# Regrouping the transfers of an FFT stage in an S4D-plus-GLU kernel

## The chip, the cores and the metric

The kernel runs on one core of a Trainium2 chip. The metric is the device time of one execution in microseconds (us); the time before is the median of three runs. Each profile is one execution recorded by the hardware profiler; times inside it are counted from its first instruction.

## The reference

The input is u (1 x 2048 x 448). It is normalized over its 448 columns and goes into two branches, whose sum with u is the output: an S4D layer (a convolution of 2048 positions, made as a product of spectra, with kernels K made from 256 complex exponentials per column) and a GLU.

```python
x  = A_u
xn = _layernorm(x, axis=-1)

# branch A
dt = jnp.exp(log_dt)
A  = -jnp.exp(log_A_real) + 1j * A_imag
C  = (C_real + 1j * C_imag) * dt[:, None]
P  = jnp.exp((A * dt[:, None])[:, :, None] * pos[None, None, :])
K  = 2.0 * jnp.einsum("dn,dnl->dl", C, P).real          # 448 x 2048
y  = irfft(rfft(xn_t, 2 * L) * rfft(K, 2 * L), 2 * L)[:, :, :L]
a  = y + xn * D_skip

# branch B, F = 1792
g  = xn @ w_gate
b  = (sigmoid(g) * (xn @ w_up)) @ w_down

return x + a + b
```

## The kernel before

Two generators run interleaved, `conv()` (branch A) and `glu()` (branch B). A loop at the end of the kernel always advances the one that has used less of its planned weight (`yield` returns a weight), so the GLU's matmuls fill the gaps that branch A leaves on TensorE. A scheduler in the framework then places the instructions of each engine; `issue_after` and `high_priority` steer it. Each engine works through its own list in order.

Branch A has three parts.

1. `prep` and `x_spec`/`pair_first` (the first 200 us and some of the middle): the parameters, and the first stage of the transform of x, whose rows go to `x1_d` in DRAM: 64 row groups (32 frequencies k, cosine and sine), 64 blocks, 448 columns. The columns of the table `wx` decide in which order the groups lie.
2. `kgen` (to about 580 us): the kernels K in 56 chunks, with a first transform stage (`first_stage`) every four chunks. Its result `sk` (14 banks of 32 columns) goes to `sk_d` in DRAM, by a store in ScalarE's queue (L540).
3. `spectra` (from about 557 us, matmuls from 587 us): the second stage of both transforms, the product, and the way back. It is in two halves of 224 columns (h) with 8 steps each (k in steps of four), 16 steps in all.

A step n of `spectra` does this:

- `back(*prev)` on the products of the step before: 8 matmuls into two PSUM tiles `pv` (L880), two ScalarE copies into `vt` (L886) and four stores of `vt` into `v_d` in DRAM, issued by SyncE (L892);
- `there`: for two pairs of frequencies, matmuls with the kernel rows `skl` and the x rows `sx` against a table `tb` (L854), one ScalarE copy `kc` (L862) and VectorE's complex product into `yy` (L865 to L868);
- `loads` of the step three ahead (`NLD = 3` buffers), issued by SyncE: two loads of x rows `sx` (L826, L827), the table `tb` (L829) and the kernel rows `skl` (L831);
- `turned` (L898): the load of a finished block of `v_d` into `vp`, turned so that positions lie on partitions. `vp` has one buffer for each half in turn, filled by eight such loads;
- once a half is complete, `last(h, m)`: the last stage, 64 matmuls for each two of its four parts m (L909), whose results VectorE adds to `ac` (the first 1024 positions) and `accs` (the others) (L917). `out` (L220) then stores rows to the output, its issues dealt round to SyncE, ScalarE and GpSimd.

For half 0, `last` runs within the steps of half 1; `due` holds the step. For half 1 it comes at the end, behind the last GLU matmuls.

The rotation of the stores, the place of `last` and the dealing are these lines:

```python
                t = wait.pop(0)
                turned(*t)
                if t == (0, 28):
                    due = [n + 1]
```

```python
            eng = (nc.sync, nc.scalar, nc.gpsimd)[outs[0] % 3]
```

The GLU's weights for its last groups are loaded and split by GpSimd (L608, L734, L735, L757, L758); its matmuls are L674 (gate and up) and L781 (down), its ScalarE and VectorE parts L682, L690, L685 and L692.

Of the kernel before, what the change touches and what calls it, by code (L numbers as in the profile page):

```python
# [11 lines left out]
F32 = mybir.dt.float32  # L12
# [8 lines left out]
D = 448  # L21
N = 256
F = 1792
NA = 32
NB = 64
NK1 = 32
# [13 lines left out]
H = D // 2  # L40
# [15 lines left out]
def _tables():  # L56

    a = np.arange(NA)[:, None]
    b = np.arange(NB)[:, None]
    k1 = np.arange(NK1)[None, :]  # L60
    ang = 2 * np.pi * ((a * (4 * k1 + 1)) % 128) / 128.0

    wk = np.zeros((4, NA, 2, 2, NK1))
    wx = np.zeros((4, NA, 2, NK1))
    for j in range(4):
        wk[j, :, 0, j % 2] = wx[j, :, 0] = np.cos(ang)
        wk[j, :, 1, j % 2] = wx[j, :, 1] = -np.sin(ang)

    k2 = np.arange(64)[None, :]
    tab = np.zeros((NK1, 128, 128))  # L70
    for q in range(NK1):
        al = 2 * np.pi * ((b * (4 * q + 1 + 128 * k2)) % 8192) / 8192.0
        c, s = np.cos(al), np.sin(al)
        tab[q] = np.block([[c, -s], [s, c]])
    tab = tab.reshape(8, 4, 128, 128).transpose(0, 2, 1, 3)

    al = 2 * np.pi * ((b * k2) % 64) / 64.0
    split = lambda t: t.reshape(64, 2, 32).transpose(0, 2, 1)
    both = lambda r, i: np.stack([split(r), split(i)], 3).reshape(64, 128)
    bk = np.zeros((2, 64, 2, 128))  # L80
    bk[:, :, 0] = both(np.cos(al).T, np.sin(al).T)
    bk[:, :, 1] = both(-np.sin(al).T, np.cos(al).T)

    wf = np.zeros((2, 2, 4, 8, 32, NA))
    l = 64 * np.arange(NA)[None] + np.arange(64)[:, None]
    for k in range(NK1):
        al = 2 * np.pi * (((4 * k + 1) * l) % 8192) / 8192.0
        wf[:, 0, k % 4, k // 4] = (np.cos(al) / L).reshape(2, 32, NA)
        wf[:, 1, k % 4, k // 4] = (-np.sin(al) / L).reshape(2, 32, NA)

    sel = np.zeros((128, 2, 2, DC, 32))
    st = np.arange(32) + 0.5
    for e in range(DC):
        for i in range(2):
            sel[DC * i + e, 0, 0, e] = st
            sel[64 + DC * i + e, 0, 1, e] = st
            sel[64 + DC * (2 + i) + e, 0, 1, e] = 1.0
    sel[:, 1] = -sel[:, 0]
    for row, tb_, sg in ((16, 1, -1.0), (32, 0, 1.0), (96, 1, 1.0), (97, 0, -1.0)):
        sel[row, 0, tb_] = sg * MAGIC  # L100
    f = lambda v, s: np.ascontiguousarray(v.reshape(s).astype(np.float32))
    return {
        "c_wk": f(wk, (128, 2, 64)),
        "c_wx": f(wx, (128, 64)),
        "c_tab": f(tab, (8, 128, 4, 128)),
        "c_bk": f(bk, (128, 2, 128)),
        "c_wf": f(wf, (128, 32, NA)),
        "c_sel": f(sel, (128, 2, 512)),
        "c_id": np.eye(128, dtype=np.float32),
    }  # L110
# [3 lines left out]
def s4d_glu_kernel(ctx, tc, io):  # L114
    nc = tc.nc
# [6 lines left out]
    dram = ctx.enter_context(tc.tile_pool(name="dram", bufs=1, space=DRAM))  # L122
    acc_d = dram.tile([128, 8, D], F32, name="acc_d")
    ph_d = dram.tile([D, 6, N], F32, name="ph_d")
    x1_d = dram.tile([64, NB, D], F32, name="x1_d")
    sk_d = dram.tile([128, D // 32, 32, 32], F32, name="sk_d")
    wt_d = dram.tile([2, NFT, 128, 8 * 128], F32, name="wt_d")

    v_d = dram.tile([2, 128, 32, H], F32, name="v_d")
    dt_d = dram.tile([2, NFT, 128, D], F32, name="dt_d")  # L130

    const = ctx.enter_context(tc.tile_pool(name="const", bufs=1, side="left"))
# [1 line left out]
    wx = const.tile([128, 64], F32, name="wx")  # L134
    wk = const.tile([128, 2, 128], F32, name="wk")[:, :, :64]
# [75 lines left out]
    def blocks(t, g, b0, nb):  # L211
        return t[g, :, b0 // 8, b0 // 4 % 2, b0 % 4 : b0 % 4 + nb]

    def out(src, b0, h):

        ds = slice(H * h, H * h + H)
        for g in range(4):
            eng = (nc.sync, nc.scalar, nc.gpsimd)[outs[0] % 3]
            outs[0] += 1
            eng.dma_start(blocks(out_t, g, b0, 4)[:, :, ds], src[32 * g : 32 * g + 32, :, ds])  # L220

# [203 lines left out]
    def kgen(pk):  # L425
# [11 lines left out]
        tl = {n: pk.tile(sh, dt_, name=n) for n, sh, dt_ in late}  # L437
# [83 lines left out]
        def first_stage(bank):  # L521

            ks, sk = tl["ks"], tl["sk"].rearrange("p k (s r j) -> p r k s j", r=2, j=2)

            pss = [
                psc[-1].tile([128, 8, 2, 32], F32, name="kp", bufs=1),
                psg.tile([128, 8, 2, 32], F32, name="kq", tag="gu", bufs=4),
            ]
            for s_ in range(8):
                for cc in range(2):  # L530
                    for r in range(2):
                        rows = slice(64 * r, 64 * r + 64)
                        nc.tensor.matmul(
                            pss[r][64 * cc : 64 * cc + 64, s_].rearrange("p j k -> p (j k)"),
                            ks[rows, s_], wk[rows, cc], start=True, stop=True,
                            skip_group_check=True,
                        )
            for r in range(2):
                nc.scalar.copy(sk[:, r], pss[r].rearrange("p s j k -> p k s j"))
            nc.scalar.dma_start(sk_d[:, bank], tl["sk"])  # L540

        with hp(HP):
            phase_load(0)
# [8 lines left out]
        for g in range(NCK // NCH):  # L552
            for c in range(NCH):
# [23 lines left out]
                for q in range(2):  # L577
                    sl = 2 * (cn % 4) + q
                    for k in range(4):
                        h, cc = k // 2, k % 2  # L580
# [222 lines left out]
    def spectra(pf):  # L803
# [18 lines left out]
        def loads(h, k):  # L822
            sx = pf.tile([128, 4, H], F32, name="sx", bufs=NLD)
            sk = pf.tile([128, 7, 4, 32], F32, name="skl", bufs=NLD)
            ds, gs = slice(H * h, H * h + H), slice(7 * h, 7 * h + 7)
            nc.sync.dma_start(sx[0:64], x1_d[k : k + 4, :, ds].rearrange("k b d -> b k d"))  # L826
            nc.sync.dma_start(sx[64:128], x1_d[32 + k : 36 + k, :, ds].rearrange("k b d -> b k d"))  # L827
            tb = pf.tile([128, 4, 128], F32, name="tb", bufs=NLD)
            nc.sync.dma_start(tb, io["c_tab"][k // 4])  # L829

            nc.sync.dma_start(sk, sk_d[:, gs, k : k + 4])  # L831
            return tb, sk, sx

        def bank(name):
# [37 lines left out]
        def back(h, k, ys_):  # L872
            vt = work("vt", [128, 2, 2, H], 2)
            pvs = [bank("pv") for _ in range(2)]
            with after():
                for j in range(2):
                    for e in range(2):
                        for i in range(2):
                            s = slice(64 * i, 64 * i + 64)
                            mm = nc.tensor.matmul(  # L880
                                pvs[i][:, j], bk[s, e], ys_[j][s, e], start=(e == 0), stop=(e == 1),
                                skip_group_check=True,
                            )
            sp_mm[:] = [mm]
            for i in range(2):
                nc.scalar.copy(vt[:, i], pvs[i])  # L886

            for j in range(2):
                for i in range(2):
                    k1 = k + 2 * j + i  # L890
                    to = v_d[h, 8 * (k1 % 4) + k1 // 4 :: 32]
                    nc.sync.dma_start(to.rearrange("r w d -> w r d"), vt[:, i, j])  # L892

        def turned(h, k):
            if h not in vp:
                vp[h] = pf.tile([128, 32, H], F32, name="vp", bufs=1)
            s = slice(k // 4, 128, 8)
            nc.sync.dma_start(vp[h][s], v_d[h, s])  # L898

        def last(h, m):  # L900

            pos = [bank("pv") for _ in range(2)]
            for i in range(2):
                for g in range(4):
                    for b in range(2):
                        s = slice(64 * b, 64 * b + 64)
                        w = 8 * g + m + i
                        with after():
                            mm = nc.tensor.matmul(  # L909
                                pos[b][32 * g : 32 * g + 32, i], wf[s, w], vp[h][s, w],  # L910
                                start=True, stop=True, skip_group_check=True,
                            )
            sp_mm[:] = [mm]
            for b in range(2):
                q, o, ds = 2 * (m // 4) + b, m % 4, slice(H * h, H * h + H)
                acc = ac[:, 4 * q + o : 4 * q + o + 2, ds] if q < 2 else accs[q][:, o : o + 2, ds]
                v.tensor_tensor(acc, acc, pos[b], ALU.add)  # L917
            if m % 4 == 2 and m < 4:
                for q in range(2):
                    out(ac[:, 4 * q : 4 * q + 4], 4 * q, h)  # L920

        ac = acl[0]
        lasts.append(last)
# [7 lines left out]
        for n, (h, k) in enumerate(steps):  # L931
# [18 lines left out]
            while len(wait) > 1 and not (due and wait[0][0] == 1):  # L950
                t = wait.pop(0)
                turned(*t)
                if t == (0, 28):
                    due = [n + 1]
            prev = (h, k, cur)
            glu_on[:] = [1]
            yield WS
# [141 lines left out]
```

## Time and profile before

| | us |
|---|---|
| median of 3 runs | 773.14 (771.35 to 775.21) |
| time of the profiled execution | 770.64 |
| span of the profile (first to last instruction) | 768.9 |
| TensorE busy | 705.4 |
| VectorE busy | 557.4 |
| ScalarE busy | 420.3 |
| GpSimd busy | 359.7 |
| TensorE clock granted, mean | 0.968 of full |

Of the 770.64 us, 1.7 lie outside the span. The transfers move 114.31 MB in 89,575 packets; SyncE's queue carries 92.36 MB of them, ScalarE's 14.57 and GpSimd's 6.17.

How to read the rows quoted below: a timeline row has the start, the time taken, the engine (a "q" behind the engine's name: an instruction of its queue that issues a transfer), the line, the operation and its tiles, the count, and in brackets the idle time before it and what ended it. DVE is VectorE, ACT ScalarE, POOL GpSimd, SP SyncE, PE TensorE.

### The profile page before, as it was taken

What the parts mean: (1) busy time and instruction counts of PE and PEld (TensorE: products, weight loads), DVE (VectorE), ACT (ScalarE), POOL (GpSimd) and SP (SyncE); (2) the same over time, 40 slices, a digit from 0 to 9 for tenths busy, and PEclk for the clock granted to TensorE, in tenths of its full rate; (3) what the DMA queues carried; (4) which work ended last, traced back from release to release, by engine and by line L of the source; (5) the groups of instructions that cost most, each with busy time, mean ns of one, the idle gap of its engine ahead of it and who ended that gap; (6) DMA issues with size and microseconds to landing.
All of it is one profiled execution on the core that took longest, in us unless ns stands there. A gap on an engine that the chain in (4) does not pass through costs nothing.

```text
span 768.9 us, 19294 instructions
## 1 busy us (share of the span) xinstructions
PE 705.4 (92%) x7868; PEld 555.6 (72%) x7868; DVE 557.4 (72%) x768; ACT 420.3 (55%) x647; POOL 359.7 (47%) x423
## 2 busy tenths in 40 slices
PE   2798899997999999898999999999899999969994
PEld 1575688876877877565788887887777778746783
DVE  5779996798978998778478977877864554634553
ACT  3636364767677976777387667686552322312320
POOL 1101036896785788853437584486555002331001
PEclk9998899999999999899999999999999999989998
DMA  9936337334323542363962232222157999999846
GB/s 205 227 81 187 95 93 230 101 122 151 120 70 126 185 135 67 108 189 92 269 182 69 68 124 66 90 94 67 41 142 199 283 240 238 230 241 242 189 127 161
DMA packets 89575, 114.31 MB, mean 149 GB/s; under 512 B 10896, under 2 KB 77456, under 8 KB 89232
## 3 DMA queue, kind: packets, MB, share of 16 engines
q1 hardware_dynamic: 80176, 92.36, 45.3%
q10 hardware_dynamic: 6736, 14.57, 6.3%
q0 software_dynamic: 2576, 6.17, 3.1%
q8 instruction: 62, 1.02, 0.6%
q14 instruction: 25, 0.20, 0.1%
HBM read 69.21 MB, written 43.84 MB: 147 GB/s over the span
## 4 chain that ended last, share of the span: by engine, by line
PE 40%; DMA 16%; DVE 15%; ACT 10%; POOL 9%; issue 7%; SPq 2%; ACTq 1%; POOLq 0%; DVEq 0%
PE gu L674 13%; PE po L781 11%; PE tr L506 4%; PE sp L854 4%; PE ko L582 3%; POOL me L483 3%; PE pv L880 2%; DVE pm L420 2%; DMA sx<-x_d 2%; DVE Et L569 2%; DVE Et L568 2%; ACT S L518 2%; POOL mf L483 2%; DVE Ft L570 2%; ACT S L516 1%
## 5 line engine op out<-in xcount | busy, mean ns | idle before, releaser
L483 POOL TENSOR_TENSOR me<-me,pm 128x32 f32<-128x32 f32 (+1 forms) x168 | 135.5, 807 | 99.5 <-DVE Et L569 88.1
L483 POOL TENSOR_TENSOR mf<-mf,pm 128x64 f32<-128x64 f32 (+1 forms) x112 | 118.0, 1054 | 4.5
L674 PE MATMUL gu<-xh,wh 128*128 128x512 f32 x336 | 101.3, 408 | 5.2 <-ACT xh L201 5.2
L569 DVE TENSOR_TENSOR Et<-me,S 128x1024 f32<-128x1024 f32 x56 | 80.0, 1429 | 24.5 <-ACT me L496 20.0
L674 PE MATMUL gu<-xh,wl 128*128 128x512 f32 x336 | 96.9, 394 | 0.0
L674 PE MATMUL gu<-xl,wh 128*128 128x512 f32 x336 | 96.6, 391 | 0.0
L781 PE MATMUL po<-dh,hh 128*128 128x448 f32 x224 | 87.3, 390 | 4.4 <-DVE acc L786 2.5
L568 DVE TENSOR_TENSOR Et<-me,S 128x1024 f32<-128x1024 f32 x56 | 77.9, 1391 | 16.8 <-ACT S L518 16.6
L690 ACT CAST hh<-hf 128x512 fp32r<-128x512 f32 x56 | 34.9, 623 | 98.9 <-DVE hf L685 74.7
L570 DVE TENSOR_TENSOR Ft<-mf,S 128x1024 f32<-128x1024 f32 x56 | 80.2, 1433 | 9.6 <-ACT S L518 7.4
L781 PE MATMUL po<-dl,hh 128*128 128x448 f32 x224 | 84.7, 379 | 0.0
L781 PE MATMUL po<-dh,hl 128*128 128x448 f32 x224 | 83.7, 376 | 0.0
L515 ACT ACTIVATE S<-tr 128x1024 f32<-128x1024 f32 x56 | 57.6, 1028 | 40.4 <-PE tr L506 34.9
L674 PEld LDWEIGHTS gu<-xh,wh 128*128 128x128 f32 x336 | 62.4, 193 | 22.1 <-ACT xh L201 6.7
L582 PEld LDWEIGHTS ko<-Et,Ft 128*32 128x32 f32 x3584 | 54.8, 112 | 28.4 <-issue 13.7
L674 PEld LDWEIGHTS gu<-xh,wl 128*128 128x128 f32 x336 | 63.2, 189 | 15.2 <-DVE pl L289 0.7
L674 PEld LDWEIGHTS gu<-xl,wh 128*128 128x128 f32 x336 | 63.2, 188 | 14.1 <-issue 0.7
L582 PE MATMUL ko<-Et,Ft 128*32 128x64 f32 x3584 | 64.9, 224 | 9.1 <-DVE Et L568 7.3
L685 DVE SCALAR_TENSOR_TENSOR hf<-th,gu 128x512 f32<-128x512 f32 x56 | 38.1, 681 | 42.3 <-PE gu L674 31.5
L506 PE MATMUL tr<-sel,ph 128*128 128x512 f32 x224 | 66.8, 419 | 1.7 <-ACT S L517 1.1
L786 DVE SCALAR_TENSOR_TENSOR acc<-po,acc 128x448 f32<-128x448 f32 x80 | 48.2, 617 | 24.4 <-PE po L781 24.3
L518 ACT ACTIVATE S<-S,hpi 128x1024 f32<-128x1024 f32 x56 | 65.5, 1169 | 0.0
(190 smaller groups left out, 1299.8 us busy)
## 6 DMA issues: line engine op xcount, KB each, us to landing
sk_d<-sk ACTq DMA_DIRECT2D x14, 512.0 KB
sx<-x_d SPq DMA_DIRECT2D x32, 224.0 KB
skl<-sk_d SPq DMA_DIRECT2D x16, 448.0 KB
v_d<-vt SPq DMA_DIRECT2D x64, 112.0 KB
vp<-v_d SPq DMA_DIRECT2D x16, 448.0 KB
wt_d<-wh SPq DMA_DIRECT2D x9, 512.0 KB
wt_d<-wl SPq DMA_DIRECT2D x9, 512.0 KB
wh<-wt_d SPq DMA_DIRECT2D x9, 512.0 KB
```

What stands on the lines that cost most here:

```text
L483: ins = nc.gpsimd.tensor_tensor(m[:, :, w + a : 2 * w : n], m[:, :, a:w:n], par(base + i).unsqueeze(2).to_broadcast([128, 4 * DC, w // n]) ...
L506: nc.tensor.matmul(ps[:, h], ph[:, cn % 2, 128 * h : 128 * h + 128], sel[:, i], start=(i == 0), stop=(i == 1),)
L515: nc.scalar.activation(rows(cs), pv, AF.Abs)
L518: sins[:] = [nc.scalar.activation(cs, cs, AF.Sin, scale=-TWO_PI, bias=hpi)]
L568: v.tensor_tensor(Et[:, :, :, 32:64], two(me[:, :, 32:64]), S[:, 1::-1], ALU.mult)
L569: v.tensor_tensor(Et[:, :, :, 0:32], two(me[:, :, 0:32]), S[:, 1:3, :, ::-1], ALU.mult)
L570: fts[:] = [v.tensor_tensor(Ft, two(mf), S[:, 3:5], ALU.mult)]
L582: mm = nc.tensor.matmul(ko[32 * j : 32 * j + 32, sl], Ft[:, cc, DC * h + 4 * q + j], Et[:, cc, DC * h + 4 * q + j], start=(k == 0), stop=( ...
L674: glu_mm[:] = [nc.tensor.matmul(ps, a_, b_, start=(n == 0), stop=(n == len(mm) - 1))]
L685: marks[1] = v.scalar_tensor_tensor(hf, th, 1.0, pgu[1], ALU.add, ALU.mult)
L781: glu_mm[:] = [nc.tensor.matmul(po, a_[:, bs], w_, start=(n == 0), stop=(n == 3 * fc - 1))]
L786: v.scalar_tensor_tensor(acc[:, b], po, 0.5, acc[:, b], ALU.mult, ALU.add)
```

## The change

- `v_d` gets the layout [half, block, q, r, 32, columns]. The table `bk` has its columns in another order, so that the partitions of `vt` are (r, w); `vt` is written as [j, i]. The four stores of a step become one of 128 partitions x 4 x 224, and ScalarE issues it, right behind its two copies to `vt`.
- The rows in `x1_d` lie as (k, c) instead of (c, k), by the table `wx`; the two loads of x become one of 128 partitions.
- `sk_d` is laid out by half and step. A load of kernel rows is one contiguous row of 3,584 bytes per partition instead of 7 pieces of 512 bytes; the store of a bank (L540) becomes 8 pieces of 512 bytes per partition instead of one of 4,096.
- `turned` reads four q x four r rows of 28,672 bytes, as large as before.
- The outs of half 0's `ac` rows all go to SyncE; those of half 1 are dealt as before.
- `due` is one step later: the last stage of half 0 moves from the steps n = 10 and 11 to n = 11 and 12.

Bytes, matmuls and the elements that the engines compute are the same.

```diff
     wk = np.zeros((4, NA, 2, 2, NK1))
-    wx = np.zeros((4, NA, 2, NK1))
+    wx = np.zeros((4, NA, NK1, 2))
     for j in range(4):
-        wk[j, :, 0, j % 2] = wx[j, :, 0] = np.cos(ang)
-        wk[j, :, 1, j % 2] = wx[j, :, 1] = -np.sin(ang)
+        wk[j, :, 0, j % 2] = wx[j, :, :, 0] = np.cos(ang)
+        wk[j, :, 1, j % 2] = wx[j, :, :, 1] = -np.sin(ang)
...
-    split = lambda t: t.reshape(64, 2, 32).transpose(0, 2, 1)
-    both = lambda r, i: np.stack([split(r), split(i)], 3).reshape(64, 128)
+    both = lambda r, i: np.stack([r.reshape(64, 2, 32), i.reshape(64, 2, 32)], 2).reshape(64, 128)
...
-    sk_d = dram.tile([128, D // 32, 32, 32], F32, name="sk_d")
+    sk_d = dram.tile([128, 2, 8, D // 64, 4, 32], F32, name="sk_d")
-    v_d = dram.tile([2, 128, 32, H], F32, name="v_d")
+    v_d = dram.tile([2, 8, 4, 4, 32, H], F32, name="v_d")
...
-    def out(src, b0, h):
+    def out(src, b0, h, engs=(nc.sync, nc.scalar, nc.gpsimd)):
         ds = slice(H * h, H * h + H)
         for g in range(4):
-            eng = (nc.sync, nc.scalar, nc.gpsimd)[outs[0] % 3]
+            eng = engs[outs[0] % len(engs)]
...
-            nc.scalar.dma_start(sk_d[:, bank], tl["sk"])
+            to = sk_d[:, bank // 7, :, bank % 7].rearrange("p e k d -> p e (k d)")
+            nc.scalar.dma_start(to, tl["sk"].rearrange("p (e k) d -> p e (k d)", k=4))
...
-            ds, gs = slice(H * h, H * h + H), slice(7 * h, 7 * h + 7)
-            nc.sync.dma_start(sx[0:64], x1_d[k : k + 4, :, ds].rearrange("k b d -> b k d"))
-            nc.sync.dma_start(sx[64:128], x1_d[32 + k : 36 + k, :, ds].rearrange("k b d -> b k d"))
+            ds = slice(H * h, H * h + H)
+            rows = x1_d.rearrange("(k c) b d -> (c b) k d", c=2)
+            nc.sync.dma_start(sx, rows[:, k : k + 4, ds])
             tb = pf.tile([128, 4, 128], F32, name="tb", bufs=NLD)
             nc.sync.dma_start(tb, io["c_tab"][k // 4])
-            nc.sync.dma_start(sk, sk_d[:, gs, k : k + 4])
+            nc.sync.dma_start(sk, sk_d[:, h, k // 4])
...
             for i in range(2):
-                nc.scalar.copy(vt[:, i], pvs[i])
-            for j in range(2):
-                for i in range(2):
-                    k1 = k + 2 * j + i
-                    to = v_d[h, 8 * (k1 % 4) + k1 // 4 :: 32]
-                    nc.sync.dma_start(to.rearrange("r w d -> w r d"), vt[:, i, j])
+                nc.scalar.copy(vt[:, :, i], pvs[i])
+            to = v_d[h, k // 4].rearrange("q r w d -> (r w) q d")
+            nc.scalar.dma_start(to, vt.rearrange("p j i d -> p (j i) d"))
...
-            s = slice(k // 4, 128, 8)
-            nc.sync.dma_start(vp[h][s], v_d[h, s])
+            src = v_d[h, k // 4].rearrange("q r w d -> r q (w d)")
+            nc.sync.dma_start(vp[h][k // 4 :: 8].rearrange("p w d -> p (w d)"), src)
...
-                    out(ac[:, 4 * q : 4 * q + 4], 4 * q, h)
+                    out(ac[:, 4 * q : 4 * q + 4], 4 * q, h, *([] if h else [[nc.sync]]))
...
                 if t == (0, 28):
-                    due = [n + 1]
+                    due = [n + 2]
```

## The prediction

> **What bounds the kernel now.** I read the page's busy times, then the stretches of the last 170 us (the only part whose order of work changes), then what TensorE waited for there, then the timelines of TensorE, ScalarE and SyncE around the longest wait, and the chain of waits for what a transfer takes.
>
> ```profile
> span 768.9 us, 19294 instructions
> ## 1 busy us (share of the span) xinstructions
> PE 705.4 (92%) x7868; PEld 555.6 (72%) x7868; DVE 557.4 (72%) x768; ACT 420.3 (55%) x647; POOL 359.7 (47%) x423
> ```
>
> TensorE is busy for 92% of the span, so only its idle time can be won. By stretch (length, TensorE busy with its count, granted clock, share of the transfer engines, GB/s):
>
> ```profile
> 600.00:660.00 60.00, 60.00 (x444) 1.00 1.09 243
> 660.00:680.00 20.00, 19.58 (x149) 1.00 1.05 233
> 680.00:700.00 20.00, 12.11 (x120) 0.83 1.01 252
> 700.00:720.00 20.00, 19.45 (x187) 1.00 0.94 222
> 720.00:740.00 20.00, 20.00 (x156) 1.00 0.58 148
> ```
>
> The transfer engines are full from 600 to 700 us, yet TensorE doesn't stop until 680; there it loses 7.89 us of 20. Its waits after 580 us (total, times, longest):
>
> ```profile
> PE pv L909 <- DMA vp<-v_d: 7.3, 1, 7.3
> PE pv L880 <- DMA bk<-in_c_bk_dram: 1.4, 1, 1.4
> PE sp L854 <- ACT vt L886: 1.1, 1, 1.1
> PE pv L909 <- issue: 0.9, 1, 0.9
> PE pv L909 <- DVE pd L866: 0.6, 1, 0.6
> ```
>
> So one wait matters: the last stage of the first half of the columns (L909) stands for the transfer of vp. TensorE's timeline (start, us, what) shows where:
>
> ```profile
> 656.90 1.78 PE L880 MATMUL pv<-yy,bk 64*128 64x224 f32 x16
> ...
> 667.01 1.78 PE L880 MATMUL pv<-yy,bk 64*128 64x224 f32 x16
> ...
> 674.62 1.78 PE L880 MATMUL pv<-yy,bk 64*128 64x224 f32 x16
> ...
> 678.66 0.93 PE L854 MATMUL sp<-sx,tb 128*64 128x224 f32 x8
> 686.84 3.26 PE L909 MATMUL pv<-vp,wf 64*32 64x224 f32 x64 [7.25 <-DMA vp<-v_d]
> ...
> 701.43 1.72 PE L909 MATMUL pv<-vp,wf 64*32 64x224 f32 x48
> 703.70 0.96 PE L909 MATMUL pv<-vp,wf 64*32 64x224 f32 x16 [0.56 <-DVE pd L866]
> ```
>
> The same 64 matmuls cost 3.26 us behind the wait, where the clock fell to 0.83, but 48 of them 1.72 us later, which is 2.29 for 64: the wait also costs 0.97 of clock. ScalarE shows the third piece:
>
> ```profile
> 658.72 0.97 ACT L886 COPY vt<-pv 128x448 f32<-128x448 f32 x2 [0.37 <-PE pv L880]
> ...
> 692.92 5.21 ACTq L220 DMA_DIRECT2D out_dram<-ac  x3
> 698.17 0.62 ACT L690 CAST hh<-hf 128x512 fp32r<-128x512 f32 x1 [18.72 <-DMA out_dram<-ac]
> ```
>
> Three stores of out stand in ScalarE's queue, wait for the late last stage, and hold up the copies behind them; that is the 1.06 us TensorE waits for vt (1.1 in the list).
>
> And SyncE shows why vp was late:
>
> ```profile
> 666.56 3.51 SPq L892 DMA_DIRECT2D v_d<-vt  x4
> ...
> 675.96 0.51 SPq L898 DMA_DIRECT2D vp<-v_d  x1
> ...
> 745.55 2.46 SPq L892 DMA_DIRECT2D v_d<-vt  x4
> 748.06 0.60 SPq L220 DMA_DIRECT2D out_dram<-acc  x1
> 750.22 0.54 SPq L898 DMA_DIRECT2D vp<-v_d  x1
> ```
>
> The last block of the first half was in vt at 659.69 (658.72 + 0.97). SyncE, busy in order with the loads of later steps, issued its four stores 6.87 us later, from 666.56, and its load, behind the next step's loads, at 675.96; it landed 10.88 us after that, at 686.84. In the chain of waits, from issue to landing:
>
> ```profile
> 659.16 6.77 DMA v_d<-vt
> ...
> 666.00 8.57 DMA vp<-v_d
> ```
>
> **The change part by part.**
>
> *Later last stage.* The last stage of half 0 moves one step on: in the changed order, 22 gate matmuls, the backward matmuls and the next forward matmuls come first. That stretch is what lies between 656.90 and 667.01, so TensorE arrives at 679.59 + 10.11 = 689.7, where before it arrived at 679.59. Even with the old transfers (landed 686.84) the wait would be gone. Removed: 7.25 of wait and 0.97 of clock. What is late next at this place is a PSUM bank: the first 64 matmuls then meet VectorE's reads as the second 64 did, so I add 0.56 once more; the bounds are 0 and twice that.
>
> *Store of v from ScalarE.* Per step, four issues leave SyncE and one appears on ScalarE, between the copies to vt and the copy kc. An issue there costs:
>
> ```profile
> L540 ACTq DMA_DIRECT2D sk_d<-sk x14: 326/327/375, 191.5 to 583.0; - x14
> ```
>
> So 0.33 us, 16 times 5.2 us on ScalarE. Behind it wait kc, then VectorE's products, then the next backward matmuls. VectorE can't begin before the matmuls on x are done, one group after those that kc reads, and this covers most of 0.33. VectorE's slack is thinnest where few GLU matmuls fill a step:
>
> ```profile
> 673.85 0.39 DVE L868 TENSOR_TENSOR yy<-pd 128x224 f32<-128x224 f32 x1
> ```
>
> It ends 0.38 us before the matmuls at 674.62, and the second half of those is needed still later. I take 0.2 in all, with 0 and 5.2 (no cover at all) as the bounds.
>
> The store also has a wait of its own. In both orders each transfer of SyncE and ScalarE waits for the one eight places earlier, and with five transfers a step instead of nine that is, for a store of v in the first half, the vp load of two steps earlier. From one store to the end of that load: 0.33 + 6.77 + 0.51 + 8.57 = 16.2 us, with the slow load of 10.88 18.5 us. Two steps (656.90 to 674.62) are 17.72 us. So a store blocks ScalarE by 0 to 0.8 us, at most six times: 0 to 4.7 us, and it must still eat through the slack above. I take 0.4.
>
> *Outs of half 0 from SyncE alone.* Three issues leave ScalarE's queue and two GpSimd's: the 1.06 us go. SyncE then issues eight in a row behind the last stage; only the loads of the sixteenth step and the second half's vp stand behind them. Even ten us of that are free: that step's forward matmuls come more than three steps later, 26.6 us at 17.72 for two. Nothing added.
>
> *SyncE's own order* becomes: kernel rows, vp, x, table. The x load now stands behind a load that waits for the store of v, landing 0.97 + 0.33 + 6.77 = 8.1 us after the backward matmuls. The x load is used three steps after those (26.6 at 8.86 a step); 26.6 - 8.1 - 0.5 leaves 18 us for a transfer, where vp's took 8.57. Hidden.
>
> *Row sizes.* A kernel load is 128 rows of 3,584 B instead of 896 of 512 B, for 512-byte rows in the 14 stores of sk, which run while the engines are half idle. No row of before separates transfers by row size, so I take nothing: below, 16 loads quicker by some tenths each that TensorE doesn't wait for; above, the same in the stores.
>
> [...]
>
> *End.* The last vp is issued at 750.22, after four stores that took 2.46 us to issue. One store from ScalarE, ready with the copies, should free 0.5 of the 0.86 us that the last stage waits ("issue" 0.9 in the list); bounds 0 and 0.86.
>
> *bk.* Its load (1.4) has somewhat fewer SyncE transfers beside it; I take 0, bounds 0 and 1.4.
>
> Sum: -7.25 - 0.97 - 1.06 + 0.56 + 0.2 + 0.4 - 0.5 = -8.6 us. The profiled run took 770.64 us (span 768.9); the runs shown have a median of 773.14 (771.35 to 775.21), so against the median **764.5 us**.
>
> **The rivals.**
>
> *1. Late loads.* The new order on SyncE delays x and the table more than they can bear. For it: the queue is a chain in which each waits for a landing. Against: 18 us of room. It needs landings twice as long; then about half of the gain goes: **769**.
>
> *2. The transfer engines are the bound.* The share of 1.05 to 1.09 up to 680 means that they lag, and the wait at L909 is only where the lag shows; bytes don't change, so 7.25 and 0.97 come back at the loads of the next steps, and 1.06 alone is won: **772**. Against: TensorE's list holds not one wait on x, table or kernel rows, and the engines have 0.06 and 0.42 of two 20-us stretches free right after, 9.6 us.
>
> *3. Slower: ScalarE blocks on its stores.* The loop store, vp load, next-but-one store closes over ScalarE's queue. It decides once store plus load exceed two steps, 17.72 us. If whole stores of 448 KB take twice 6.77, the loop takes 0.33 + 13.54 + 0.51 + 8.57 = 22.95 us, 2.6 us more a step, and with six such steps 15.7 us: 764.5 + 15.7 = **780**. For it: the loop stands at 16.2 already. Against: the four stores of before shared SyncE's queue with all loads, and the same bytes landed in 6.77.
>
> **How the numbers follow.** Forecast 0.74, late loads 0.07, full engines 0.10, blocked ScalarE 0.09. The forecast's own range is 761.6 (no bank wait, nothing on ScalarE, the end and bk at their best: 0.56 + 0.6 + 0.36 + 1.4 less) to 768 (3.5 us more on ScalarE, whose bounds allow 9.3). With two us of scatter of the runs and the late loads, 760.5 to 770 holds 8 in 10. About 0.5% (3.9 us) is what a measurement of this kernel can tell from no change: faster 0.78 (the forecast and half of the late loads), same 0.13, slower 0.09.
>
> **What would show it.** Right: TensorE's waits after 595 us name no vp before the end; in 680 to 700 us it is busy for over 19 us at a clock of 1.00; SyncE issues the eighth vp before 670 us; ScalarE has no idle time ended by a transfer; the waits on a PSUM bank at the last stage are about 0.6 twice. Wrong: idle time of ScalarE at vt or kc that is ended by vp or v_d (rival 3), waits of the forward matmuls on x, table or kernel rows (rivals 1 and 2).

## The result, and the profile after

The changed kernel takes 807.19 us (805.45 to 810.48, 4 runs) beside 773.79 us of the kernel before (771.35 to 775.21, 4 runs): a ratio of 1.044, 95% interval 1.0395 to 1.0485. The forecast was 764.5. The profiled execution took 806.23 us. In the changed kernel the load of vp is L894, the store of v L888, the last stage L905 and the outs L219.

The page after, first lines:

```profile
span 804.4 us, 19179 instructions
...
PE 718.4 (89%) x7868; PEld 560.5 (70%) x7868; DVE 560.5 (70%) x768; ACT 420.1 (52%) x647; POOL 358.8 (45%) x421
```

TensorE has 13.0 us more of busy time for the same 7868 matmuls (its mean granted clock was 0.947, against 0.968), and 22.5 us more of idle time (804.4 - 718.4 = 86.0, against 63.5). Nearly all of both lies behind 600 us, as the stretches show (length, busy time with its count of each engine, sums, granted clock, share of the transfer engines, GB/s):

```profile
600.00:680.00 80.00, 71.68 (x476) 53.18 (x472) 36.06 (x70) 16.26 (x32) 9.32 (x11) 0.91 0.78 186
680.00:740.00 60.00, 52.07 (x440) 37.36 (x440) 29.37 (x56) 14.77 (x29) 11.01 (x13) 0.94 0.77 201
740.00:804.00 64.00, 40.71 (x350) 31.63 (x346) 21.56 (x42) 7.08 (x14) 4.42 (x8) 0.81 0.40 122
```

From 600 to 680 us before had TensorE at work for 60.00 + 19.58 us, with the transfer engines at a share of 1.09 and 1.05. Now they carry less, 0.78 and 186 GB/s, and TensorE stands all the same: over all 16 engines together it isn't that there is too much to move. Waits after 540 us, of TensorE, then of VectorE, of ScalarE, and of SyncE's queue (total, times, longest):

```profile
PE pv L880 <- DVE yy L867: 12.7, 7, 4.0
PE pv L905 <- DMA out_dram<-acc: 12.5, 1, 12.5
PE sp L854 <- ACT vt L886: 3.4, 2, 2.3
PE pv L880 <- DVE yy L868: 2.2, 2, 1.7
```

```profile
DVE yy L865 <- ACT kc L862: 65.4, 13, 9.1
```

```profile
ACT kc L862 <- DMA vp<-v_d: 16.7, 3, 6.4
```

```profile
SPq L894 <- DMA v_d<-vt: 87.0, 12, 24.9
```

The 7.3 us of the last stage on vp are gone. In their place TensorE waits nine times, 14.9 us, for VectorE's products, VectorE for ScalarE's kc, and kc for a load of vp that it doesn't read: its engine stood before the issue of a store. ScalarE's timeline has the place:

```profile
647.73 0.97 ACT L886 COPY vt<-pv 128x448 f32<-128x448 f32 x2 [6.34 <-PE pv L880]
654.61 0.37 ACTq L888 DMA_DIRECT2D v_d<-vt  x1
655.08 0.97 ACT L862 COPY kc<-sp 128x448 f32<-128x448 f32 x2 [6.38 <-DMA vp<-v_d]
```

The store could have left at 648.70; it left at 654.61, and kc behind it. The chain of waits gives the loop and its terms (start, time taken, what):

```profile
616.33 3.22 DMA v_d<-vt
...
619.57 20.31 DMA vp<-v_d
...
639.95 5.16 DMA v_d<-vt
...
645.13 20.11 DMA vp<-v_d
...
665.32 6.12 DMA v_d<-vt
...
671.45 23.01 DMA vp<-v_d
...
694.54 0.37 ACTq L888
...
739.36 19.29 DMA v_d<-vt
```

Store, load, next-but-one store: 616.33, 639.95, 665.32, 694.54. Each of the last three stores left as the load of vp eight places ahead of it in the two queues had landed (619.57 + 20.31 = 639.88, 645.13 + 20.11 = 665.24, 671.45 + 23.01 = 694.46); in before the load of the table at 674.59 stands in the same way behind the load of vp at 666.00 (666.00 + 8.57 = 674.57). A loop takes 26.07 us on average, where two steps of before took 17.72. Three loops cost 3 x 8.35 = 25.1 us; in the second half the slow store at 739.36 holds vt for 7.3 us, and at the end the last stage waits 12.5. Less the 7.25 + 0.97 + 1.06 that did go, that makes 35.6, and the two profiled executions differ by 806.23 - 770.64 = 35.6. That it comes out to the tenth is luck: the terms are waits of different engines (of the 7.3 us at vt TensorE lost 2.3), and the lower clock behind the waits has no term of its own. The row of the 12.5 us names a store of out, which the last stage doesn't read; it reads the last block of vp, whose load left at 777.01 and whose rows, by the trace's records of single rows, moved until 789.17. That this load set the wait is the likely reading; the row doesn't show it.

The 20.1 to 23.0 us of a vp load, where before had 8.57, are the new fact. They are the time from issue to landing, and the loads come in pairs. SyncE's timeline has the first pair:

```profile
616.47 0.54 SPq L894 DMA_DIRECT2D vp<-v_d  x1
...
619.57 0.53 SPq L894 DMA_DIRECT2D vp<-v_d  x1
```

By the records of single rows, the first of these loads moved from 619.09 to 629.98, and the second began at 632.32 and moved for 7.0 us. The other two pairs look the same: the second load's own rows took 8.5 and 10.9 us, where three loads of before took 6.0 to 6.6. So a third to a half of the 20 us is the load itself, and most of the rest is spent behind the vp load that was issued 3.1 to 3.3 us ahead of it.

At the end of each kernel a load of vp is nearly alone. The stretches (columns as in the prediction), first of before, then of after:

```profile
751.50:753.50 2.00, 2.00 (x12) 1.00 0.97 229
```

```profile
784.00:789.00 5.00, 0.00 (x0) 0.50 0.23 92
```

The same 448 KB keep 0.97 x 16 = 15.5 transfer engines busy before and 0.23 x 16 = 3.7 after. Such a share counts a row's whole time in the stretch in which the row starts, so it gives the count only where the stretch holds that time (a quarter of a microsecond of before, from 751.50, shows 5.85). The records of single rows agree with the count: before, 16 rows start within 0.6 us and take 1.3 to 2.4 us each, so 16 are under way at once; after, never more than four are in this stretch, and each new one starts as another ends. The new load reads its 16 rows in two dimensions, four r and four q, that can't be merged into one; before read them in one dimension of 16.

So the first theory, A: the outer dimension of the load's source sets how many transfer engines carry it, here four. The rivals: B, the single store of v, or its place in ScalarE's queue, is what costs, as the prediction's third rival had it; and C, any read order other than that of DRAM is slow, however many engines it uses.

### The profile page after: what moved, and what is told of

Its sections match the earlier page's. It is cut to its first block, busy times and chain, and to the rows that moved or that the text cites. A ratio compares the mean times of both kernels' runs of the same rounds, so it can differ in the third digit from the quotient of the medians.

```text
span 804.4 us, 19179 instructions
## 1 busy us (share of the span) xinstructions
PE 718.4 (89%) x7868; PEld 560.5 (70%) x7868; DVE 560.5 (70%) x768; ACT 420.1 (52%) x647; POOL 358.8 (45%) x421
## 4 chain that ended last, share of the span: by engine, by line
PE 39%; DMA 21%; DVE 14%; POOL 9%; ACT 8%; issue 7%; SPq 1%; ACTq 1%; POOLq 0%; DVEq 0%
PE gu L674 16%; PE po L781 9%; DMA vp<-v_d 8%; DMA v_d<-vt 4%; PE tr L505 4%; POOL me L482 4%; PE ko L582 3%; POOL mf L482 2%; PE sp L854 2%; DVE pm L419 2%; PE pv L880 2%; DVE Et L568 2%; DVE Et L569 2%; ACT S L517 2%; DVE Ft L570 1%
## 5 line engine op out<-in xcount | busy, mean ns | idle before, releaser
L674 PEld LDWEIGHTS gu<-xh,wl 128*128 128x128 f32 x336 | 63.5, 190 | 15.3 <-DVE pl L288 0.7
L865 DVE TENSOR_TENSOR yy<-kc,sp 128x448 f32<-128x448 f32 x32 | 19.7, 616 | 75.0 <-ACT kc L862 65.4
```

What stands on the lines that cost most here:

```text
L674: glu_mm[:] = [nc.tensor.matmul(ps, a_, b_, start=(n == 0), stop=(n == len(mm) - 1))]
```

## Experiments

**The read order alone, taken back and put in.** In the changed kernel the load reads its rows in DRAM's order:

```diff
-            src = v_d[h, k // 4].rearrange("q r w d -> r q (w d)")
+            src = v_d[h, k // 4].rearrange("q r w d -> (q r) (w d)")
```

> The changed kernel, but the vp load reads its 16 rows of 28,672 bytes in the order in which they lie in DRAM (one dimension of 16) instead of in the order r, q (4 x 4, which don't merge into one). Bytes, row sizes, queues and waits are the same; the rows land on other partitions, so the result is permuted. Theory A (a load whose source is 4 x 4 rows is served by 4 of the 16 engines, each with four rows one behind the other; this makes vp's 20 us and, through the wait of v's store for the load two steps earlier, blocks ScalarE): vp lands in 6 to 11 us, ScalarE isn't stopped by a transfer, 762 to 768 us. Theory B (stores of v in ScalarE's queue are slow to land or block it by themselves, whatever the load does): no change against the changed kernel, 800 to 808 us.

Measured: 768.08 us (761.61 to 770.31, 10 runs), ratio to before 0.993 (0.9895 to 0.9965): the upper end of what A expected. TensorE's waits after 540 us:

```profile
PE pv L880 <- DVE yy L868: 2.6, 2, 1.3
PE ko L582 <- DVE Et L568: 2.5, 1, 2.5
PE pv L880 <- DMA bk<-in_c_bk_dram: 2.1, 1, 2.1
PE pv L905 <- DVE pd L866: 0.5, 2, 0.3
```

39 us come back by the order of 16 rows. The waits for products are down to 2.6 us from 12.7 + 2.2, and none names a transfer of v; no wait of ScalarE's names a transfer either. The store still stands in ScalarE's queue, so B is not what costs 33 us. Then the reverse, in the kernel before:

```diff
-            nc.sync.dma_start(vp[h][s], v_d[h, s])
+            src = v_d[h].rearrange("(r q e) w d -> e q r (w d)", r=4, q=4)[k // 4]
+            nc.sync.dma_start(vp[h][s].rearrange("p w d -> p (w d)"), src)
```

> The kernel before, but its vp load takes the same 16 rows in the order q, r (4 x 4, not mergeable); the result is permuted, nothing else is changed: stores of v from SyncE, last stage at its old place. Theory A: vp takes about 20 us instead of 8.6 to 10.9, the wait at the last stage grows from 7 to 18 us or more, and SyncE, which waits eight transfers back, holds up loads too: 785 to 810 us. Theory B: 773 us, no change, since no store is in ScalarE's queue.

Measured: 831.35 us (827.2 to 834.29, 4 runs), ratio 1.0742 (1.0674 to 1.081): the order alone, with nothing else of the change, costs more than the whole change did. The direction is A's; the size was missed by over 20 us, and the wait for vp at the last stage of the first half stayed near its 7.25 us instead of growing to 18. TensorE's largest waits, and ScalarE's:

```profile
PE pv L910 <- DMA out_dram<-acc: 25.3, 1, 25.3
PE sp L854 <- ACT vt L886: 21.7, 7, 5.9
PE pv L910 <- DMA vp<-v_d: 7.5, 1, 7.5
```

```profile
ACT vt L886 <- DMA v_d<-vt: 57.2, 8, 10.6
```

Here nothing of ScalarE's stands behind a store. The stores themselves land late (8.23 to 12.08 us in the chain of waits, against 6.77 in before), and vt's buffers come free late. The one vp load in that chain takes 11.27 us, not the 20 that A expected.

**How many engines.** Two more read orders in the changed kernel, first 8 x 2, then 2 x 8:

```diff
-            src = v_d[h, k // 4].rearrange("q r w d -> r q (w d)")
+            src = v_d[h, k // 4].rearrange("q r w d -> (q r) (w d)").rearrange("(a b) x -> b a x", a=2)
```

> The changed kernel with the vp load reading the 16 rows in an 8 x 2 order instead of 4 x 4 (the result is permuted by it). Theory A (the size of the outer dimension of the source sets how many of the 16 transfer engines carry the load: 4 with 4 x 4, 8 with 8 x 2): 2 rows for an engine instead of 4, a load of some 9 to 13 us, a total of 768 to 778. Theory B (any order other than that of DRAM is slow, by two dimensions as such): 800 to 808, with loads of 20 us.

> The changed kernel with the vp load reading the 16 rows in a 2 x 8 order instead of 4 x 4 (the result is permuted by it). Theory A (the size of the outer dimension of the source sets how many transfer engines carry the load: 16, 8, 4 and here 2): 8 rows for an engine, a load of some 35 to 45 us where 8 x 2 took 9.5 in the chain of waits and 4 x 4 took 20.1 to 23.0, a loop of some 20 to 25 us a step and a total of 880 to 980. Theory B (4 x 4 is slow for another reason, such as the distance of 28,672 bytes between the rows that follow each other): at most as slow as 4 x 4, 807 or less.

Measured: 8 x 2 took 770.29 us (one run, before 773.34), within A's 768 to 778; 2 x 8 took 841.75 us (one run, before 770.89). The chain of waits of 8 x 2, then of 2 x 8:

```profile
667.65 9.50 DMA vp<-v_d
```

```profile
606.60 11.85 DMA v_d<-vt
618.46 14.05 DMA vp<-v_d
...
678.44 16.28 DMA vp<-v_d
694.80 16.31 DMA v_d<-vt
```

And a stretch at the end of 2 x 8, in which only rows of vp move:

```profile
810.00:812.00 2.00, 0.00 (x0) 0.50 0.13 57
```

0.13 x 16 = 2.1 engines, against 3.7 with 4 x 4 and 15.5 with one dimension of 16. For 8 x 2 the last load of vp shows it by its rows, which start in two groups:

```profile
748.50:749.00 0.50, 0.50 (x4) 1.00 1.83 459
749.00:749.90 0.90, 0.90 (x6) 1.00 0.00 0
749.90:751.00 1.10, 1.10 (x7) 1.00 0.88 209
```

459 GB/s for 0.50 us and 209 for 1.10 are 8 rows of 28,672 bytes each; the second eight start as the first eight end. So 8 engines carry it. This is A's count in all four orders, and C falls: 8 x 2 is no more in DRAM's order than 4 x 4, and its one time is within the runs of the load in DRAM's order (761.61 to 770.31). But the total of 2 x 8 was expected at 880 to 980, from loads of 35 to 45 us; they took 14 to 16. In these stretches an engine moved more where few ran: 57 GB/s / 2.1 = 27 GB/s each, 92 / 3.7 = 25, but 229 / 15.5 = 14.8. A single row took 1.06 us with two under way and 1.07 with four, but 1.9 with eight and with sixteen. From the start of its first row to the end of its last, a load with almost nothing beside it took 2.6 us on 16 engines, 4.3 on 8, 5.4 on 4 and 8.6 on 2. From 8 to 4 that is 1.1 us more, while in the loop the one stopped ScalarE once, for 4.3 us, and cost nothing that its time shows, and the other cost 33 us: the count alone doesn't price the loss. What the other transfers add on the few engines that the load uses was not measured apart. And with two engines more of the loop sits in the stores, 11.85 to 16.31 us here against 3.22 to 6.12 with 4 x 4: each row of the chain counts the time to its own landing, and what one kernel books on the load the other books on the store.

What is shown is the count for four orders of this one load: 16, 8, 4 and 2 rows under way at once, with an outer dimension of 16, 8, 4 and 2. What sets it for other transfers was not shown.

**Who passes it on.** The changed kernel with its 4 x 4 load, the store moved to SyncE:

```diff
-            nc.scalar.dma_start(to, vt.rearrange("p j i d -> p (j i) d"))
+            nc.sync.dma_start(to, vt.rearrange("p j i d -> p (j i) d"))
```

> The changed kernel with its 4 x 4 load of vp, but the store of v issued by SyncE. Theory A (the load alone is the cause; the store in ScalarE's queue is only the place where its slowness is passed on): no gain or a small one, 795 to 815, and the idle time ended by v_d or vp is found at vt or at the forward matmuls instead of at kc. Theory B (the prediction's third rival as written: ScalarE blocks because its store waits for a load two steps back, and without that the slow load hides): kc no longer waits for vp, 765 to 780.

Measured: 837.92 us (one run, before 770.89). Both were wrong on the size; of A's signs, the idle time at vt that a store of v ends is there. With this load the store was cheaper in ScalarE's queue than in SyncE's, by 30 us. TensorE's and ScalarE's waits:

```profile
PE pv L905 <- DMA out_dram<-acc: 26.2, 1, 26.2
PE sp L854 <- DMA tb<-in_c_tab_dram: 16.1, 4, 7.0
PE sp L854 <- issue: 14.5, 2, 7.6
```

```profile
ACT vt L886 <- DMA v_d<-vt: 63.3, 8, 10.0
```

Now that SyncE issues store and load, the tables of later steps come late: the prediction's first rival, which the change as it stands did not show. With a load that uses all engines, does the store's queue matter at all? Both of these give v the old order of `bk`, rows (r, q), one store of 32 x 16 x 224 a step and a load of 16 rows; they differ in the engine that issues the store:

```diff
-            to = v_d[h, k // 4].rearrange("q r w d -> (r w) q d")
-            nc.scalar.dma_start(to, vt.rearrange("p j i d -> p (j i) d"))
+            to = v_d[h, k // 4].rearrange("r q w d -> w r q d")
+            nc.sync.dma_start(to, vt.rearrange("p j i d -> p (j i) d"))
...
-            src = v_d[h, k // 4].rearrange("q r w d -> r q (w d)")
+            src = v_d[h, k // 4].rearrange("r q w d -> (r q) (w d)")
```

> The changed kernel with a store and a load of v that both go over 16 rows: v_d is written as (r, q) rows in the old order of bk, one store a step of 32 x 16 x 224, issued by SyncE and not by ScalarE; the load of vp reads 16 rows in their order. Theory A (the 4 x 4 read order of the vp load is what cost, and a store in ScalarE's queue some us besides): as fast as the changed kernel with v's transfers as before, 760 to 763 us, no idle time of ScalarE ended by a transfer. Theory B (one large store a step is itself slow, wherever it stands): 768 or more, with landings of the store well over the 6.77 us of the four small ones.

> The same kernel as the one with a single store of 32 x 16 x 224 from SyncE, but with the store issued by ScalarE. Theory A (ScalarE's queue, where the store stands ahead of kc, costs some us): 765 to 768 us, 4 to 6 above the one from SyncE, with TensorE waiting for VectorE's products. Theory B (the layout of the store matters and its queue does not): the same as from SyncE within 2 us.

Measured: from SyncE 764.84 us (756.07 to 766.59, 6 runs), ratio 0.9877 (0.9834 to 0.9919); from ScalarE 765.66 us (762.07 to 770.94, 9 runs), ratio 0.9909 (0.9877 to 0.994). The intervals overlap: a single store in ScalarE's queue costs nothing that these runs can tell, and the 4 to 6 us that were expected for it are not there. 764.84 lies between what A and B expected for the store from SyncE (760 to 763, and 768 or more), so it decides less than the pair does. Four stores in that queue are another matter. This version keeps the new order of `bk`, and has four stores a step by r and a load of 16 rows:

```diff
-            nc.scalar.dma_start(to, vt.rearrange("p j i d -> p (j i) d"))
+            for r in range(4):
+                to = v_d[h, k // 4, r].rearrange("q w d -> w q d")
+                nc.scalar.dma_start(to, vt[32 * r : 32 * r + 32].rearrange("p j i d -> p (j i) d"))
```

> The changed kernel, correct, with rows in DRAM in the order r, q: the load is 16 rows in one dimension, and the store of a step becomes four (one for each r) of 32 partitions x 4 x 224, still from ScalarE. Theory A: 763 to 770 us; four issues cost ScalarE 1.5 us a step, mostly covered. Theory B: at or above the changed kernel, 800 us or more, since ScalarE now has four stores a step to wait with.

Measured: 776.45 us (773.23 to 783.52, 10 runs), ratio 1.0063 (1.0021 to 1.0104), outside both expectations. TensorE's wait, and ScalarE's timeline:

```profile
PE pv L880 <- DVE yy L867: 6.5, 6, 2.4
```

```profile
657.22 3.36 ACTq L889 DMA_DIRECT2D v_d<-vt  x4
660.67 0.97 ACT L862 COPY kc<-sp 128x448 f32<-128x448 f32 x2 [3.49 <-issue]
```

Four issues and their waits take 3.4 us ahead of kc, where one takes 0.37: VectorE's slack covers the one and not the four.

**The other parts of the change.** All of it but v's transfers:

> The changed kernel with its v part undone (layout, table order, four stores a step from SyncE, load of 16 rows as before); merged load of x, large kernel rows, outs from SyncE and the later last stage stay. Theory A and theory B both say that the loss goes: the 7.25 us wait, its 0.97 us of clock and ScalarE's 1.06 us are won, 762 to 768 us. If one of the other parts costs by itself (theory C: 512-byte stores of sk, or SyncE's outs), it stays above 773.

Measured: 761.58 us (761.21 to 768.28, 4 runs), ratio 0.9865 (0.9797 to 0.9932). That another part of the change costs (theory C) is not borne out. Then its two parts alone, first the last stage and the outs (the new parameter of `out` and its call are as in the change):

```diff
-            eng = (nc.sync, nc.scalar, nc.gpsimd)[outs[0] % 3]
+            eng = engs[outs[0] % len(engs)]
...
-                    due = [n + 1]
+                    due = [n + 2]
```

> The kernel before with only two edits of the change: the last stage of half 0 one step later, and the outs of half 0 from SyncE alone. All transfers are as before. The prediction's terms for these two were -7.25 - 0.97 - 1.06 + 0.56 = -8.7 us: 764.4 against the median of 773.1 shown there, 762 to 767. Rival (full transfer engines, the prediction's second rival): the time comes back at later loads, 770 to 772.

Measured: 766.92 us (760.09 to 775.7, 12 runs), ratio 0.992 (0.9886 to 0.9953). The last stage no longer waits for vp, and the interval leaves out the rival's 770 to 772. Then the loads alone (the `loads`, `wx` and `sk_d` parts of the diff), and of these the kernel rows alone:

> The kernel before with only the regrouped loads of x and of the kernel rows (with their layouts in DRAM); v's transfers, the last stage and the outs are as before. The prediction took nothing for these: 773, within 3 us of before, TensorE still waiting some 7 us for vp at the last stage of the first half. Rival (fewer instructions in SyncE's queue let the vp load leave earlier and shorten that wait, which is what the version with v's transfers as before had over the one with only the later last stage, 761.6 against 766.9): 766 to 769, with that wait at 4 or less.

> The kernel before with the kernel rows alone regrouped: a load is one row of 3,584 bytes a partition instead of seven of 512, and the store of a bank has pieces of 512 bytes; the two loads of x, v, the last stage and the outs are as before. Theory A (512-byte rows kept the transfer engines busy longer for the same bytes, and the wait for vp at the last stage came of that): share of the transfer engines from 600 to 680 us at 0.90 as in the version with both loads regrouped, where before had 1.08; the wait for vp gone or under 2 us; 763 to 767 against a before of 771 to 773. Theory B (fewer issues in SyncE's queue let vp leave earlier): share still above 1.0, the wait for vp still 5 us or more, 770 to 774.

Measured: both loads 764.68 us (759.11 to 769.39, 12 runs), ratio 0.9916 (0.9884 to 0.9948); kernel rows alone 765.76 us (760.91 to 769.73, 12 runs), ratio 0.9929 (0.9895 to 0.9964). In both the wait for vp is gone; the prediction had given them nothing. The stretch from 600 to 680 us, of the version with both, of that with the kernel rows alone, and of the later last stage:

```profile
600.00:680.00 80.00, 79.00 (x579) 1.00 0.89 255
```

```profile
600.00:680.00 80.00, 80.00 (x592) 1.00 1.06 266
```

```profile
600.00:680.00 80.00, 80.00 (x590) 1.00 1.08 257
```

The kernel rows alone give the time of theory A without its sign, a share of 0.90: it stayed at 1.06, as B had it, while B's time and its wait did not come. SyncE's timeline there has the eighth load of vp:

```profile
669.46 0.51 SPq L899 DMA_DIRECT2D vp<-v_d  x1
```

That is 6.5 us earlier than the 675.96 of before, with as many issues in the queue as before. But one profile each can't put this down to the rows: counted from its first backward matmuls, the eighth load left after 81.87 us in before, after 74.78 here, and after 76.73 in the version with the later last stage alone, whose loads are those of before. How larger rows win their 5.3 us is open. And a share of 1.06 to 1.08 doesn't mean that the engines are full: 266 and 257 GB/s pass at 1.06 and 1.08, and 255 at 0.89.

The two parts take away the same wait, and don't add up: 6.4 us of the medians for the later last stage, 6.2 for the loads, and together, in the version with all but v's transfers, 9.6. The versions at 0.9865 and 0.9877 beat both kernels, by about 1%; which of the two is the quicker these runs don't tell.

## Why the prediction was wrong

**The step that failed** is the sizing of the load in "The store also has a wait of its own": 0.33 + 6.77 + 0.51 + 8.57 = 16.2 us. The 8.57 us were carried over from a load of 16 rows in one dimension to one of four by four rows, because bytes and row size are the same. The load took 20.1 to 23.0 us from issue to landing: 7.0 to 10.9 for its own rows on four engines, and most of the rest behind the vp load just ahead of it, which the sum had no term for though two steps hold two loads. The store took 3.2 to 6.1, less than the 6.77 counted. With these the loop is 26.07, not 16.2. The bounds given for the term, 0 to 4.7 us, stood on a load of at most 10.88 us, the slowest of before, and no row of before had a load with another order of its dimensions. That order had to be named as a thing that no row showed, and bounded.

**The third rival had the mechanism, not the cause.** The loop over ScalarE's queue closed as described, and its sign (ScalarE idle at kc, ended by vp) is in the list of waits. It was priced by a doubled store, at 780 and with a chance of 0.09; what grew was the load. ScalarE's queue was only the place where a slow load became visible: with the read order taken back the store in that queue costs none of the 33 us, and with the store on SyncE the loss is larger.

**Later last stage and outs**: -7.25 - 0.97 - 1.06 + 0.56 = -8.7 us forecast; alone they measured 773.34 - 766.92 = 6.4 us, with an interval of the ratio that reaches from 3.6 to 8.8. Right in kind, at the edge in size. The second wait on a PSUM bank (0.56) did not come.

**The issue on ScalarE** (0.2 us): not contradicted. One issue takes 0.37 us in the profile, and the versions with the store on either engine can't be told apart; but their intervals are 5 to 7 us wide, and with the read order taken back TensorE waits 2.6 us for VectorE's products, where before names no such wait.

**Row sizes** (nothing taken, gains of "some tenths" thought possible): wrong as a statement on the kernel before, where the kernel rows alone are worth 5.3 us of the medians (interval of the ratio 0.9895 to 0.9964). How much it would have added to the sum is not settled: they win the same wait as the later last stage, and both together gave 9.6 us of the medians, the later last stage alone 6.4. The rate in the stretch from 600 to 680 us, 243 and 233 GB/s in before, was 266 with the larger rows, but 257 also where the 512-byte rows stayed, so it doesn't show what the size of a row is worth.

**Full transfer engines** (second rival): refuted. With the later last stage alone the share stays at 1.08 from 600 to 680 us, and TensorE loses nothing there.

**SyncE's own order, the end, bk**: 18 us of room for the x load held in the changed kernel, whose TensorE has no wait on x, table or kernel rows. The end went the other way: 12.5 us of wait where 0.5 of 0.86 was to be won, most likely by the same slow load.

Without the failed step the direction of the forecast stands, and its size in part. The forecast is a ratio of 764.5 / 773.14 = 0.9888. The changed kernel with the read order alone put right has 0.993, whose interval (0.9895 to 0.9965) leaves the forecast out: 3.1 us of the medians and not 8.6. The versions with both sides of v over 16 rows have 0.9877 and 0.9909, with the forecast inside; they write v in another way than the change did.

## What to carry to other kernels

When a transfer is regrouped, look at the order and size of its dimensions and not at its bytes and row size alone: an outer dimension of 4 that can't be merged with the next gave the whole load of this kernel to 4 of 16 transfer engines (3.7 by the share) and turned a gain of about 1% (a ratio of 0.993) into a loss of 4% (1.044). Read the share of the transfer engines in a stretch in which that one transfer moves steadily; times 16 it gave the count here (15.5, 3.7 and 2.1). And a chain that closes over a queue is to be priced with each of its terms grown, not only with the one that changes hands.

## What the runs showed of the hardware

For the load of vp the number of transfer engines went with the outer dimension of its source: 16, 8, 4 and 2 rows under way at once for sources of 16, 8 x 2, 4 x 4 and 2 x 8 rows, and shares of 0.97, 0.23 and 0.13 for the first and the last two. With almost nothing beside the load the loss was less than in proportion (2.6, 4.3, 5.4 and 8.6 us for all its rows): a row of 28,672 bytes took 1.9 us with 16 or 8 under way, and 1.07 and 1.06 us with 4 and 2.

Loads of vp on four engines stood one behind the other: in three pairs issued 3.1 to 3.3 us apart the second began 2.3 to 2.5 us after the last row of the first had ended (629.98 and 632.32 in the first pair). The store of a step took 3.22 to 6.12 us in the chain of the first half of the changed kernel, 19.29 in its second half while rows of vp loads moved (from 732.79 to 757.30; it held vt's buffer for 7.3 us), and 11.85 to 16.31 in the first half with loads on two engines. That the loads made these stores late is the likely reading; no run shows it apart.
